# Layer 1 of a fused attention and feed-forward kernel: features and attention take one ring of four PSUM banks, and the second products come one chunk later

## The chip, the cores and the metric

The kernel runs on one core of one Trainium2 chip. The metric is the device time of one launch in microseconds (us); lower is better. TensorE is called PE here, its weight loads PEld, VectorE DVE, ScalarE ACT, GpSimd POOL, and SyncE, which issues the DMAs, SP.

## What is computed

Batch 4, 8 heads, 576 positions, head size 64, so 2304 tokens of width 512; both feed-forward layers are 512 to 2048 to 512.

```python
def attention(q, k, v):                 # per batch and head, m = 32 landmarks
    q_lm, k_lm = means of q, k over 18 neighbouring positions
    A  = softmax(q @ k_lm.T / 8)        # 576 x 32
    Bm = softmax(q_lm @ k_lm.T / 8)     # 32 x 32
    C  = softmax(q_lm @ k.T / 8)        # 32 x 576
    Z  = Bm.T / (norm1(Bm) * norminf(Bm) + 1e-6)
    for _ in range(6):
        Z = 2 * Z - Z @ Bm @ Z          # Newton steps towards the inverse
    return A @ Z @ C @ v

def layer1(x, w_in, w_out):             # x: heads side by side
    h = x @ w_in
    return (h * clip(h + 3, 0, 6) / 6) @ w_out

def layer2(x, w_in, w_out, a, b):
    h = x @ w_in
    P = a[0] + a[1]*h + a[2]*h**2 + a[3]*h**3
    Q = 1 + abs(b[0])*abs(h) + abs(b[1])*h**2
    return (P / (Q + 1e-6)) @ w_out

out = layer2(layer1(attention(q, k, v)))
```

## The kernel before, in words

**Weights.** They arrive as 64-bit floats. For each of 32 pieces ACT (L140) and DVE (L141 to L143) turn the bits into a 32-bit value, called `val`, and for 24 of the pieces ACT and POOL (`split`, L94 and L99) then divide it into a high and a low part. A product of two such split operands is three matmuls: high by high, high by low, low by high.

**Attention, batch by batch.** `scores_c` makes the scores of C and of Bm in four PSUM tiles (two tiles "end", two tiles "big"); DVE takes maxima (L295 to L299), makes the exponent's offset `nb` (L301), and ACT the exponentials (L307 for the big tiles). Then come transposes (`transpose_e`), the Newton steps (`first_e`, `first_v`, `newton`) and `tmat`, whose result is the small matrix `T`. `u_pair` multiplies `T` by the first layer's weights (L227) and keeps the split product `us` (L442, L443). `scores_a` and `soft_a1` to `soft_a3` make the softmax A, transposed and split, as the tile `AT`. Batch 0 goes through this ahead of layer 1; batches 1 to 3 go through it in the middle of layer 1 of the batch before.

**Layer 1.** The tokens are 8 blocks of 288; each block has 16 chunks of 128 features, 128 chunks in all. Three steps serve a chunk:

- `l1_in`: six matmuls of 288 columns (L467) into a PSUM tile `psh`; ACT makes relu(h + 3) (L470), DVE the product g (L472), which is the last reader of the PSUM tile.
- `l1_split`: ACT (L94) and POOL (L99) divide g into the tile `ghl`, 4 buffers.
- `l1_out`: twelve matmuls (L490) from `ghl` into the four accumulators `psy0` to `psy3` of the block, one bank each. When a block is done, ACT and DVE empty the four banks into `y` tiles (L514, L516, L518), of which there are 2 buffers, and DMAs store them.

**PSUM** has 8 banks here: four for `psy`, two that the attention takes in turn under the tag `psa`, and two that `l1_in` takes in turn under the tag `psh` (batch 0's attention uses both kinds). A tile waits until the last reader of the tile that had its bank before is done.

**Layer 2** works through 6 blocks of 384 tokens in an order written by hand.

**What sets the order.** Up to layer 2 every step is entered in a list with a place (`at(place, f)`); the list is sorted by place. Chunk n has `l1_in` at place n, `l1_split` at n + 1.1, `l1_out` at n + LEAD + 0.2. Buffers and banks of one tag are handed out in turn in this sorted order. A scheduler that works with its own model of the engines then decides in which order the instructions stand on each engine; each engine carries its own list out in that order, and an instruction that waits holds up those behind it.

```python
def at(place, f, *a):
    plan.append((place, len(plan), f, a))
...
for n in range(NCH):
    at(n, l1_in, n)
    at(n + 1.1, l1_split, n)
    at(n + LEAD + 0.2, l1_out, n)
```

Of the kernel before, what the change touches and what calls it, by code (L numbers as in the profile page):

```python
# [9 lines left out]
F32 = mybir.dt.float32  # L10
F32R = mybir.dt.float32r
# [14 lines left out]
P = 128  # L26
HB = S // 2
# [33 lines left out]
def fused(ctx: ExitStack, tc: tile.TileContext, qT, kT, v, w_in, w_out, w2_in, w2_out, ca, cb, out):  # L61
# [29 lines left out]
    def split(dst_hi, dst_lo, src, hi_eng, lo_eng):  # L91

        if hi_eng is A:
            A.activation(dst_hi, src, AF.Copy)  # L94
        elif hi_eng is G:
            G.tensor_scalar(dst_hi, src, 1.0, 0.0, op0=ALU.mult, op1=ALU.add)
        else:
            V.tensor_copy(dst_hi, src)
        lo_eng.tensor_tensor(dst_lo, src, dst_hi.bitcast(F32), op=ALU.subtract)  # L99
# [80 lines left out]
    w1p = pw1.__enter__()  # L180
# [3 lines left out]
    pp = ps_l1.__enter__()  # L184
# [6 lines left out]
    st = {}  # L191

    def psa(tag="psa"):
        return pp.tile([P, 512], F32, tag=tag, name=tag, bufs=2 if tag in ("psa", "psh") else 1)

    def load_kq(b, cut=1):
        kx[b] = att.tile([P, NPAIR, S + LM], F32, tag="kx", name="kx")
# [34 lines left out]
    def scores_a(b, h):  # L232
        sT = att.tile([P, 18, LM], F32, tag="sT", name="sT", bufs=1)
        pss = [psa("psh" if b == 0 else "psa") for _ in range(2)]
        by_head(
            pss, slice(0, HB),
            lambda r, a: kx[b][r:r + 64, a, S:S + LM],
            lambda r, a: qx[b][r:r + 64, a, h * HB:(h + 1) * HB],
        )
        for g in range(2):  # L240
            V.transpose(sT[:, 9 * g:9 * g + 9, :].rearrange("p a m -> p (a m)"), pss[g][:, :HB])
        st[b, h, "sT"] = sT
# [27 lines left out]
    def scores_c(b):  # L270

        qs = st.pop((b, "qs"))
        mx = att.tile([P, 2, 4], F32, tag="cmx", name="cmx", bufs=2)
        end = [psa() for _ in range(2)]
        by_head(
            end, slice(0, TN + LM),
            lambda r, a: qs[r:r + 64, a, :], lambda r, a: kx[b][r:r + 64, a, 512:S + LM],
        )
        if b == 0:
            far = end  # L280
            big = [psa("psh") for _ in range(2)]
        else:

            far = []
            for g in range(2):
                t = att.tile([P, TN + LM], F32, tag=f"ce{g}", name="ce", bufs=1)
                A.activation(t, end[g][:, 0:TN + LM], AF.Copy)
                far.append(t)
            big = [psa() for _ in range(2)]
# [158 lines left out]
    hps, ghl, yps = {}, {}, {}  # L448
# [8 lines left out]
    def l1_in(n):  # L457
        blk, c = turn[n]
        b, h = divmod(blk, 2)
        at = AT[b, h]  # L460
        f0 = (c % 4) * P
        ps = pp.tile([P, 512], F32, tag="psh", name="psh", bufs=2)
        k = 0
        for g in range(2):
            u = U[b, c // 4, g]
            for wp, xp in ((0, 0), (0, 1), (1, 0)):
                PE.matmul(ps[:, :HB], u[:, wp, f0:f0 + P], at[:, xp, g, :], start=(k == 0), stop=(k == 5))  # L467
                k += 1
        r = w1p.tile([P, HB], F32, tag="r", name="r")
        A.activation(r, ps[:, :HB], AF.Relu, bias=three)  # L470
        gg = w1p.tile([P, HB], F32, tag="g", name="g")
        V.scalar_tensor_tensor(gg, in0=r, scalar=6.0, in1=ps[:, :HB], op0=ALU.min, op1=ALU.mult)  # L472
        hps[n] = gg

    def l1_split(n):
        gg = hps.pop(n)
        t = w1p.tile([P, 2, HB], F32R, tag="ghl", name="ghl", bufs=4)
        split(t[:, 0, :], t[:, 1, :], gg, A, G)
        ghl[n] = t

    def l1_out(n):
        blk, c = turn[n]
        c0, c1 = (0, NFC - 1) if blk > 1 else (c - c % HC, c - c % HC + HC - 1)
        if c == c0:
            yps[blk] = [pp.tile([P, 512], F32, tag=f"psy{e}", name="psy") for e in range(NDC)]
        ps, t = yps[blk], ghl.pop(n)
        o = (c % 2) * DM
        for e in range(NDC):
            for i, (wp, xp) in enumerate(((0, 0), (0, 1), (1, 0))):
                PE.matmul(  # L490
                    ps[e][:, :HB], w1[c // 2][wp][:, o + e * P:o + (e + 1) * P], t[:, xp, :],
                    start=(c == c0 and i == 0), stop=(c == c1 and i == 2),
                )
        if c == c1 and c1 < NFC - 1:
            part[blk] = [slab.tile([P, GW], F32, tag="slab", name="ypart") for i in range(2)]
            for e in range(NDC):
                y = part[blk][e // 2][:, (e % 2) * HW:(e % 2) * HW + HB]
                if e % 2 == 0:
                    A.activation(y, ps[e][:, :HB], AF.Copy, scale=1.0 / 6.0)
                else:  # L500
                    V.tensor_scalar(y, ps[e][:, :HB], 1.0 / 6.0, None, op0=ALU.mult)
        elif c == c1:
            ps = yps.pop(blk)
            yd[blk] = dram.tile([P, NDC, HB], F32, name=f"yd{blk}")
            for e in range(NDC):
                if blk == 2 * B - 1 and e >= 2:
                    if e == 2:
                        y2 = w1p.tile([P, 2, HB], F32R, tag="ghl", name="y2", bufs=4)
                    y = y2[:, e - 2].bitcast(F32)
                else:  # L510
                    y = w1p.tile([P, HB], F32, tag="y", name="y")
                if blk in part:
                    y0 = part[blk][e // 2][:, (e % 2) * HW:(e % 2) * HW + HB]
                    V.scalar_tensor_tensor(y, in0=ps[e][:, :HB], scalar=1.0 / 6.0, in1=y0, op0=ALU.mult, op1=ALU.add)  # L514
                elif e % 2 == 0:
                    A.activation(y, ps[e][:, :HB], AF.Copy, scale=1.0 / 6.0)  # L516
                else:
                    V.tensor_scalar(y, ps[e][:, :HB], 1.0 / 6.0, None, op0=ALU.mult)  # L518
                SP.dma_start(yd[blk][:, e], y)
# [61 lines left out]
    def at(place, f, *a):  # L581
        plan.append((place, len(plan), f, a))
# [55 lines left out]
            at(n0 + 19.5 + 4 * u, u_pair, b, u)  # L638

    NCH = 2 * B * NFC  # L640
    LEAD = 3
    L2P = {}

    def open_l2():
# [11 lines left out]
# [4 lines that stand above are left out]
    at(NCH - 30, open_l2)  # L660
# [180 lines left out]
```

## Time and profile before

| | us |
|---|---|
| median of 3 runs (870.58, 873.90, 874.69) | 873.9 |
| the profiled execution's own time | 875.29 |
| its span, first to last instruction | 873.5 |
| PE busy within the span | 834.2 |
| DVE busy | 577.2 |
| POOL busy | 483.2 |
| ACT busy | 474.9 |

The sums of the prediction are made against the profiled execution, 875.29 us, which lies 1.4 us above the median of the runs. A busy PE is not yet a PE at its peak: matmuls overlap in a pipeline, so the time that one adds to a stream of its kind is read from how far apart their starts are. In a row of a timeline the bracket at the end is the idle time of the engine before it and what ended that idle time.

### The profile page before, as it was taken

The numbers are of one execution on the slowest core, as the hardware profiler recorded it, in microseconds if no ns is written. First come the engines' busy times: TensorE is split into PE (matmuls) and PEld (weight loads), VectorE is DVE, ScalarE is ACT, GpSimd is POOL, SyncE is SP. The second block draws the span as 40 slices with busy tenths as digits, with TensorE's granted clock in tenths as the row PEclk, the third lists the DMA queues.
The fourth block names the chain that finished last, engine by engine and source line by source line (L and its number), as shares of the span: only waits on it lengthen the run. The fifth ranks groups of instructions, "written<-read, shape, count | busy, mean of one in ns | idle before, by whom it ended". The sixth has DMA issues, their size and how long they took to land.

```text
span 873.5 us, 14948 instructions
## 1 busy us (share of the span) xinstructions
PE 834.2 (96%) x5766; PEld 748.6 (86%) x5766; DVE 577.2 (66%) x910; ACT 474.9 (54%) x876; POOL 483.2 (55%) x353
## 2 busy tenths in 40 slices
PE   9679989999999899998999999999999999999998
PEld 8558879788977789888999899898998998989986
DVE  6967895776576945766215876765766666666566
ACT  3434654465445634655434666565665655656564
POOL 1438364465345533577331886766676685675542
PEclk9768999999999999999999999999999999999999
DMA  9765464669148740595797010010010010000000
GB/s 354 275 226 168 147 229 167 225 201 334 38 158 287 253 163 28 189 327 197 262 324 254 1 37 8 30 37 1 37 37 1 37 36 1 37 1 1 37 1 36
DMA packets 46310, 113.16 MB, mean 130 GB/s; under 512 B 6176, under 2 KB 14368, under 8 KB 45856
## 3 DMA queue, kind: packets, MB, share of 16 engines
q1 hardware_dynamic: 46240, 112.22, 36.7%
q8 instruction: 45, 0.74, 0.3%
q14 instruction: 25, 0.20, 0.1%
HBM read 81.79 MB, written 30.41 MB: 128 GB/s over the span
## 4 chain that ended last, share of the span: by engine, by line
PE 66%; DVE 15%; DMA 6%; ACT 6%; issue 4%; POOL 2%; SPq 0%; DVEq 0%; ACTq 0%; POOLq 0%
PE po L740 20%; PE ph L687 20%; PE psy L490 14%; PE psh L467 7%; DMA raw<-in_moe_w_out 3%; DVE val L142 2%; DVE val L143 2%; PE psa L227 2%; DMA qx<-in_q 2%; DVE g L472 1%; ACT val L140 1%; PE psa L410 1%; DVE val L141 1%; DMA yr<-yd 1%; DMA yd<-y 1%
## 5 line engine op out<-in xcount | busy, mean ns | idle before, releaser
L490 PE MATMUL psy<-ghl,whi 128*128 128x288 f32 x1024 | 225.3, 304 | 6.7 <-POOL ghl L99 4.4
L99 POOL TENSOR_TENSOR ghl<-g,ghl 128x288 fp32r<-128x288 f32 x128 | 127.4, 999 | 151.8 <-ACT ghl L94 143.1
L740 PE MATMUL po<-w2s,g2hl 128*128 128x512 f32 x864 | 209.6, 396 | 1.5 <-POOL g2hl L99 1.5
L687 PE MATMUL ph<-yhl,w2s 128*128 128x384 f32 x1152 | 208.5, 336 | 0.6 <-DVE y L518 0.6
L687 PEld LDWEIGHTS ph<-yhl,w2s 128*128 128x128 f32 x1152 | 202.1, 188 | 4.5 <-DVE y L518 0.8
L740 PEld LDWEIGHTS po<-w2s,g2hl 128*128 128x128 f32 x864 | 161.3, 188 | 37.9 <-POOL g2hl L99 2.9
L490 PEld LDWEIGHTS psy<-ghl,whi 128*128 128x128 f32 x1024 | 169.7, 191 | 16.9 <-issue 7.3
L490 PE MATMUL psy<-ghl,wlo 128*128 128x288 f32 x512 | 150.4, 299 | 0.0
L467 PE MATMUL psh<-AT,us 128*128 128x288 f32 x768 | 134.7, 308 | 12.5 <-DVE g L472 11.4
L467 PEld LDWEIGHTS psh<-AT,us 128*128 128x128 f32 x768 | 112.9, 194 | 25.5 <-DVE g L472 16.3
L717 DVE SCALAR_TENSOR_TENSOR q<-q,r 128x768 f32<-128x768 f32 (+1 forms) x52 | 46.6, 896 | 114.2 <-ACT r L712 114.2
L699 POOL TENSOR_SCALAR q<-t,cb_s 128x768 f32<-128x768 f32 x44 | 56.5, 1283 | 100.9 <-ACT t L697 100.9
L99 POOL TENSOR_TENSOR g2hl<-g,g2hl 128x768 fp32r<-128x768 f32 (+1 forms) x52 | 89.7, 1726 | 32.4 <-ACT g2hl L94 32.4
L472 DVE SCALAR_TENSOR_TENSOR g<-r,psh 128x288 f32<-128x288 f32 x128 | 56.8, 448 | 73.4 <-ACT r L470 65.2
L94 ACT ACTIVATE ghl<-g 128x288 fp32r<-128x288 f32 x128 | 56.2, 442 | 83.1 <-DVE g L472 75.9
L490 PEld LDWEIGHTS psy<-ghl,wlo 128*128 128x128 f32 x512 | 97.8, 191 | 0.9 <-issue 0.9
L470 ACT ACTIVATE r<-psh,three 128x288 f32<-128x288 f32 x128 | 63.1, 498 | 56.8 <-PE psh L467 56.6
L711 ACT ACTIVATE r<-q,lnb 128x768 f32<-128x768 f32 (+1 forms) x52 | 46.2, 889 | 81.8 <-POOL q L700 76.3
L99 POOL TENSOR_TENSOR wlo<-val,whi 128x1024 fp32r<-128x1024 f32 x24 | 59.9, 2496 | 52.1 <-ACT whi L94 48.9
L700 POOL TENSOR_TENSOR q<-q,t 128x768 f32<-128x768 f32 x44 | 84.5, 1920 | 3.7
L697 ACT ACTIVATE t<-ph 128x384 f32<-128x384 f32 x96 | 46.9, 489 | 56.5 <-PE ph L687 55.9
L718 DVE SCALAR_TENSOR_TENSOR p<-p,ca_s,r 128x768 f32<-128x768 f32 (+1 forms) x52 | 64.6, 1243 | 0.0
(144 smaller groups left out, 1016.3 us busy)
## 6 DMA issues: line engine op xcount, KB each, us to landing
raw<-in_moe_w_in SPq DMA_DIRECT2D x32, 512.0 KB, 5.9
raw<-in_moe_w_out SPq DMA_DIRECT2D x32, 512.0 KB, 5.3
wis<-wid SPq DMA_DIRECT2D x24, 512.0 KB, 7.4
w2s<-w2di SPq DMA_DIRECT2D x16, 512.0 KB, 6.0
w2s<-w2do SPq DMA_DIRECT2D x16, 512.0 KB, 5.9
yd<-y SPq DMA_DIRECT2D x32, 144.0 KB, 2.9
out<-o SPq DMA_DIRECT2D x18, 256.0 KB, 2.0
vx<-in_v SPq DMA_DIRECT2D x4, 1024.0 KB, 8.5
```

What stands on the lines that cost most here:

```text
L94: A.activation(dst_hi, src, AF.Copy)
L99: lo_eng.tensor_tensor(dst_lo, src, dst_hi.bitcast(F32), op=ALU.subtract)
L467: PE.matmul(ps[:, :HB], u[:, wp, f0:f0 + P], at[:, xp, g, :], start=(k == 0), stop=(k == 5))
L470: A.activation(r, ps[:, :HB], AF.Relu, bias=three)
L472: V.scalar_tensor_tensor(gg, in0=r, scalar=6.0, in1=ps[:, :HB], op0=ALU.min, op1=ALU.mult)
L490: PE.matmul(ps[e][:, :HB], w1[c // 2][wp][:, o + e * P:o + (e + 1) * P], t[:, xp, :], start=(c == c0 and i == 0), stop=(c == c1 and i == 2),)
L687: PE.matmul(ps[i][:, :T2], w2i[u][wp][:, d * 256 + i * P:d * 256 + (i + 1) * P], yh[:, xp, d, :], start=(k == 0), stop=(k == 11),)
L697: A.activation(t[:, i], h, AF.Abs)
L699: eng.tensor_scalar(q[:, cs], t[:, cs], cb_s[:, 1:2], cb_s[:, 0:1], op0=ALU.mult, op1=ALU.add)
L700: eng.tensor_tensor(q[:, cs], q[:, cs], t[:, cs], op=ALU.mult)
L718: V.scalar_tensor_tensor(p, in0=p, scalar=ca_s[:, 0:1], in1=r, op0=ALU.add, op1=ALU.mult)
L740: PE.matmul(ops[j][m], t[:, xp, i, m * P:(m + 1) * P], w2o[u][wp][:, i * DM:(i + 1) * DM], start=(c == 0 and k == 0), stop=(c == NFC - 1 a ...
```

## The change

Three edits. The tiles that were tagged `psa` and `psh` now share one tag, `psx`, with 4 banks, taken in turn by all of them in the order of the sorted list. `LEAD` is 4 in place of 3, so that `l1_out` of a chunk stands one place later. The tag `ghl` has 5 buffers in place of 4.

```diff
     def psa(tag="psa"):
-        return pp.tile([P, 512], F32, tag=tag, name=tag, bufs=2 if tag in ("psa", "psh") else 1)
+        return pp.tile([P, 512], F32, tag="psx" if tag in ("psa", "psh") else tag, name=tag, bufs=4 if tag in ("psa", "psh") else 1)
...
-        ps = pp.tile([P, 512], F32, tag="psh", name="psh", bufs=2)
+        ps = psa("psh")
...
-        t = w1p.tile([P, 2, HB], F32R, tag="ghl", name="ghl", bufs=4)
+        t = w1p.tile([P, 2, HB], F32R, tag="ghl", name="ghl", bufs=5)
...
-                        y2 = w1p.tile([P, 2, HB], F32R, tag="ghl", name="y2", bufs=4)
+                        y2 = w1p.tile([P, 2, HB], F32R, tag="ghl", name="y2", bufs=5)
...
-    LEAD = 3
+    LEAD = 4
```

The number of instructions on each engine is the same; their order is not, since the scheduler sees other waits. Two places follow.

PE in the start of the program, from batch 0's second pair of transposes to the first Newton step (`warm` are matmuls without a use, L379 is `first_v`, L368 `first_e`, L398 and L401 `newton`, and L227 from qx and kx is `scores_a` of batch 0). Before:

```order
L357 MATMUL psy_315<-ident,e 128x128 x4
L379 MATMUL psh<-vx,eT 32x64 x16
L227 MATMUL psh<-qx,kx 32x288 x4
L379 MATMUL psh<-vx,eT 32x64 x4
L227 MATMUL psh<-qx,kx 32x288 x4
L592 MATMUL warm<-bm_281 128x128 x11
L368 MATMUL psa<-bm_281 128x128 x2
L379 MATMUL psh<-vx,eT 32x64 x20
L592 MATMUL warm<-bm_281 128x128 x4
L398 MATMUL psn<-ev 128x128
```

In the changed kernel:

```order
L357 MATMUL psy_315<-ident,e 128x128 x4
L592 MATMUL warm<-bm_281 128x128 x11
L368 MATMUL psa<-bm_281 128x128 x2
L379 MATMUL psh<-vx,eT 32x64 x20
L227 MATMUL psh<-qx,kx 32x288 x4
L592 MATMUL warm<-bm_281 128x128 x4
L227 MATMUL psh<-qx,kx 32x288 x4
L398 MATMUL psn<-ev 128x128
L379 MATMUL psh<-vx,eT 32x64 x20
```

Both halves of `scores_a` moved from ahead of `first_e` to behind it; the second half now takes the bank that the first `first_e` tile had.

ACT around the exponentials of batch 1 (L307), in layer 1 of batch 0 (L470 are the relus of single chunks, L94 with `ghl` the high parts, L499 empties an accumulator, L442 evicts `u_pair`). Before:

```order
L140 ACTIVATE val<-raw 128x1024
L307 ACTIVATE e,csm<-psa,cnb 128x512
L308 ACTIVATE e,csm<-ce,cnb 128x64
L307 ACTIVATE e,csm<-psa,cnb 128x512
L308 ACTIVATE e,csm<-ce,cnb 128x64
L470 ACTIVATE r<-psh,three 128x288 x2
L94 ACTIVATE ghl<-g 128x288 x2
L442 ACTIVATE us<-psa 128x512 x2
```

In the changed kernel:

```order
L470 ACTIVATE r<-psh,three 128x288 x2
L499 ACTIVATE ypart<-psy 128x288 x2
L94 ACTIVATE ghl<-g 128x288
L307 ACTIVATE e,csm<-psa,cnb 128x512
L308 ACTIVATE e,csm<-ce,cnb 128x64
L307 ACTIVATE e,csm<-psa,cnb 128x512
L308 ACTIVATE e,csm<-ce,cnb 128x64
L94 ACTIVATE ghl<-g 128x288
L442 ACTIVATE us<-psa 128x512 x2
```

The exponentials now stand behind two relus and the emptying of a finished accumulator, and PE's `u_pair` (evicted by L442), which takes over the two big score banks, stands behind 8 matmuls of one `l1_out`, 2 of the next, two `l1_in` and 10 more of `l1_out`.

## Rows read from the trace of the kernel before

**Rows 1.** Windows, three stages: stretch and length, busy us (instructions) of PE, PEld, DVE, ACT, POOL; granted clock, DMA share, GB/s.

```profile
0.00:72.00 72.00, 56.59 (x472) 46.80 (x473) 56.89 (x105) 29.23 (x58) 28.56 (x30) 0.79 0.77 282
72.00:465.00 393.00, 374.38 (x3281) 339.09 (x3279) 245.39 (x436) 202.56 (x438) 196.88 (x164) 0.99 0.60 207
465.00:873.50 408.50, 403.28 (x2016) 362.76 (x2016) 274.89 (x370) 243.14 (x380) 257.78 (x160) 1.00 0.08 28
```

**Rows 2.** Chain that ended last, in order of time: start, us, what.

```profile
413.13 1.59 PE psy L490 x12
415.52 1.59 PE psy L490 x12
...
504.77 4.19 PE po L740 x18
```

**Rows 3.** Waits of PE from 72 to 465: total us, times, longest.

```profile
PE psh L467 <- DVE g L472: 7.2, 9, 2.1
PE psy L490 <- POOL ghl L99: 4.4, 4, 2.1
```

**Rows 4.** Timeline of PE, the longest waits: start, us, what, idle before.

```profile
201.57 0.66 PE L467 MATMUL psh<-AT,us 128*128 128x288 f32 x3 [1.40 <-DVE g L472]
...
256.77 1.06 PE L467 MATMUL psh<-AT,us 128*128 128x288 f32 x6 [1.81 <-DVE g L472]
...
284.23 0.54 PE L490 MATMUL psy<-ghl,whi 128*128 128x288 f32 x2 [1.52 <-ACT y L516]
...
296.98 1.09 PE L467 MATMUL psh<-AT,us 128*128 128x288 f32 x3 [2.15 <-DVE g L472]
...
399.47 0.61 PE L490 MATMUL psy<-ghl,whi 128*128 128x288 f32 x1 [2.07 <-POOL ghl L99]
```

**Rows 5.** Windows of 20 us, columns as in rows 1.

```profile
280.00:300.00 20.00, 16.33 (x117) 14.71 (x117) 14.27 (x21) 11.52 (x29) 10.40 (x7) 0.92 0.67 242
...
400.00:420.00 20.00, 20.00 (x144) 20.00 (x143) 9.93 (x14) 10.09 (x19) 14.83 (x12) 0.93 0.66 233
```

**Rows 6.** Timeline of PE in the start of the program.

```profile
26.80 0.81 PE L227 MATMUL psh<-qx,kx 64*32 64x288 f32 x8 [1.78 <-DVE sT L241]
...
57.20 2.77 PE L467 MATMUL psh<-AT,us 128*128 128x288 f32 x10 [0.75 <-ACT us L442]
...
67.36 3.25 PE L467 MATMUL psh<-AT,us 128*128 128x288 f32 x12 [4.23 <-DVE g L472]
70.41 1.37 PE L490 MATMUL psy<-ghl,whi 128*128 128x288 f32 x5
```

**Rows 7.** Timeline of DVE in the start of the program.

```profile
32.82 1.45 DVE L141 TENSOR_SCALAR val<-val 128x1024 uint32<-128x1024 uint32 x1
...
36.53 0.74 DVE L254 TENSOR_REDUCE sm<-sT 128x18 f32<-128x576 f32 x1
37.20 1.75 DVE L347 TENSOR_SCALAR rc<-rc 128x2 f32<-128x2 f32 x1
...
40.38 0.60 DVE L370 SCALAR_TENSOR_TENSOR ev<-psa,rc,ident 128x128 f32<-128x128 f32 x2
```

**Rows 8.** Timeline of POOL in the start of the program.

```profile
31.66 2.07 POOL L248 TENSOR_TENSOR sT<-sT,mx 128x576 f32<-128x576 f32 x1 [3.08 <-DVE mx L247]
36.58 2.34 POOL L99 TENSOR_TENSOR wlo<-val,whi 128x1024 fp32r<-128x1024 f32 x1 [2.85 <-ACT whi L94]
...
43.55 1.41 POOL L99 TENSOR_TENSOR AT<-aT,AT 128x576 fp32r<-128x576 f32 x1 [1.87 <-ACT AT L94]
```

**Rows 9.** Timeline of PE, scores of batch 1 and the next `u_pair`.

```profile
88.28 1.09 PE L227 MATMUL psa<-kx,qs 64*32 64x512 f32 x16
...
97.61 1.11 PE L227 MATMUL psa<-val,T 64*32 64x256 f32 x32
```

**Rows 10.** Timeline of ACT, second large exponential of batch 1.

```profile
95.31 0.68 ACT L307 ACTIVATE e<-psa,cnb 128x512 f32<-128x512 f32 x1
```

**Rows 11.** Timeline of DVE at the end of the fourth block.

```profile
284.19 0.46 DVE L518 TENSOR_SCALAR y<-psy 128x288 f32<-128x288 f32 x1 [4.24 <-DMA yd<-y]
```

## The prediction

> **What bounds the kernel.** I read the windows by stage first. From 465 us on, in layer 2, PE is busy 403.3 of 408.5 us, and up to 72 us it has little to do [rows 1]. In layer 2 the chain of waits is PE after PE, 18 matmuls every 4.19 us [rows 2]; its order is written by hand, so those 408 us stay. What can move lies ahead of 465 us. From 72 to 465 us PE is busy 374.4 of 393 us, DVE 245, POOL 197, ACT 203 [rows 1]: PE sets the pace, at 0.133 us a matmul (12 take 1.59 us, and 2.39 us part two starts, so a chunk is 1.6 us of products and 0.8 us of features) [rows 2]. The reader is to see that at most the 18.6 idle us, and what the clock loses after them, are to be won there.
>
> Then the waits of PE in that stage: features wait 7.2 us, in nine places, until DVE's g gives a bank back, and products wait 4.4 us for POOL's low part [rows 3]. Four single waits carry most of that, and a fifth, 1.52 us, is for an accumulator to be emptied [rows 4]. Behind two of them the granted clock of a 20 us window falls to 0.92 and 0.93 [rows 5]: PE ran at 2.4 GHz, stood for 2.15 and 2.07 us [rows 4], and for a part of what followed had 1.2 GHz. At either level that is read as (1 - 0.92) x 20 = 1.6 us and 1.4 us lost.
>
> **The change, part by part.** No instruction is added or taken away, and no DMA. What changes is how long PE can go on when another engine is late. Before, between the end of a chunk's features and the next use of its bank lie two products and one chunk's features, 30 matmuls or 4.0 us; products follow three chunks behind. Now, where attention takes no tile, four products and three features lie between, 66 matmuls or 8.8 us, and products have one chunk, 2.4 us, more time. Where attention takes two tiles per chunk, as in the Newton steps, four banks reach only to the next chunk but one or less, about 2.4 us, less than before. So the two halves of the stage go different ways.
>
> *A, the start.* Half of batch 0's A scores, done at about 27.6 us before [rows 6], now need a bank that `first_e` holds until DVE evicts it, at about 41 us [rows 7]. So the softmax work on DVE and POOL moves from before the Newton steps into them. One reduction of 0.74 us leaves DVE's path to `first_e`, and POOL's 2.07 us subtraction, beside which a 1024-wide operation took 1.45 us [rows 7, 8], goes too. I take 2 us off the start of the Newton steps, give 0.5 us back within them, and get -1.5 us at the first products (70.41 us) [rows 6]. In POOL's list batch 1's three additions (L218) now all stand ahead of the first low part; I cost that at nothing, because the first g comes late anyway, and at about 2 us, by the like-sized subtraction [rows 8], if it comes early. The gain's end is the whole 4.23 us wait [rows 6]. The other end: from 27.6 us to the end of POOL's split at 44.96 us the chain took 17.4 us [rows 8]; started at 41 us it would end at 58.4 us, 1.2 us after the first features (57.20) [rows 6], and with DVE shared by the Newton steps up to +3 us.
>
> A rule speaks against this term. An update of rc, 128x2 numbers, took 1.75 us beside POOL's 2.34 us split [rows 7, 8]. The Trainium skill (SBUF — State Buffer, Terms, shared port pair) has VectorE and GpSimd locking one pair of ports for a whole instruction; now that split falls on the last step before `first_e`, and by the rule the term would be about 0 in place of -1.5 us.
>
> *B, batch 1's exponentials.* PE's `u_pair` takes the banks of the big scores, and its cover is 32 matmuls, 4.3 us. The big scores ended at 89.37 us [rows 9], the second large exponential at 96.0 us [rows 10], 6.6 us later; before, 8.2 us passed until `u_pair` [rows 9], so nothing waited. Now PE waits 6.6 - 4.3 = 2.3 us, and the next products stand behind that wait; as after 2.15 us at 296.98, the clock may fall, 1.6 us [rows 4, 5]. Sum +3.0 us, with a little under half of that for a fall that isn't certain. Ends: 0 (ACT comes earlier) and 6.6 + 1.6 = +8.2 us (the exponentials, now behind the emptying of an accumulator that ends with those 32 matmuls, leave no cover).
>
> *C, features of blocks 3 and 4.* The waits at 201.57 (1.40 us) and 256.77 (1.81 us) [rows 4]: the first goes, since the conversions are spread over more chunks there, and half the second, -2.3 us. Ends -3.2 and 0.
>
> *D, end of block 4.* DVE stood 4.24 us for the store of `y` [rows 11] and everything behind it came late: 1.52 us for the accumulator, then 2.15 us for g [rows 4]. Now more work lies between the accumulator's last and next use (0.8 us by the order), and both features that follow are ahead; the second wait and its clock loss go. -0.8 - 2.15 - 1.6 = -4.5 us. Ends -5.3 (all of the three) and 0.
>
> *E, end of block 6.* POOL is late by a burst of layer 2 splits. With 2.4 us more in hand the 2.07 us wait and about 1 us of smaller ones go (4.4 in all in the stage) [rows 3, 4], and the clock's 1.4 us [rows 5]: -4.4 us. Ends -4.5 and 0, if the burst only grows.
>
> *F, new waits.* In the Newton steps of batches 1 to 3, and at three block ends where the order leaves 0.6 to 1.0 us less before the emptied accumulator is used: nothing in the trace shows them; bounds 0 and three times 2.3 us as in B, +6.9. I take +2 us, nearer to the small end, because the features' g mostly comes within the cover left.
>
> The fifth buffer of `ghl` adds no instruction; it holds the chunk that the later products leave open, and without it POOL's low part would wait one chunk, 2.4 us, sooner. Sum: -1.5 + 3.0 - 2.3 - 4.5 - 4.4 + 2.0 = -7.7 us from 875.29 us, which is 867.6 us: **868 us**, 0.7% under the median of 873.9 us.
>
> **The rivals.**
>
> *Nothing is won.* DVE and POOL carry bursts of conversions that take as long as before; a deeper ring only lets PE run ahead and stand later, and in the busy stretches it isn't deeper at all, so the change doesn't do what it says. For it: 7.2 us of waits come only with late g, and a bank isn't their first cause [rows 3]. Against: between the bursts DVE has room, 245 of 393 us [rows 1]. Then A is 0, C -1, D and E -2 each, B and F +5: 875.3 us, by the median 874 us. The Trainium skill (TensorE: Matmul & The Clock Gate, HAM oscillation) tells of a kernel in which PSUM double-buffering on top of a steadily fed PE gave no further gain; by that rule the time stays.
>
> *Attention holds the features' banks.* In-order PE stands at each batch's exponentials until ACT and DVE have done the softmax. Place: `u_pair` behind the big scores of batch 1, and the features behind the transposes of batches 2 and 3. Price: 8.2 us once (B's end) and twice 4.2 us (the 6.6 us less a chunk's 2.4 us), 16.6 us. Against it stand C, D and E, -11.2 us, with A at 0: +5.4 us, 880 us. It decides the sign from 11.2 us of such waits on, and is over the bound below from about 14 us. For it: the long DVE list between two g in batch 1; against it: in batches 2 and 3 the order puts 4 us of products and more ahead of the transposes.
>
> *All waits go.* g's 7.2 and POOL's 4.4 us [rows 3], the clock's 3.0 us [rows 5], and no new ones: 14.6 us, 861 us.
>
> **How the numbers follow.** A measurement of this kernel can tell about 0.5% from no change, that is 869.5 to 878.3 us. Forecast (864 to 872 us) 0.42, nothing won (870 to 878 us) 0.27, attention holds the banks (876 to 886 us) 0.19, all waits go (856 to 864 us) 0.12. Four fifths of the forecast's chance and all of the last lie below 869.5 us: faster 0.46; same 0.33; slower 0.21, of which 0.16 is the second rival and 0.05 the first's upper edge with A at +3. The range, 859 to 880 us, leaves out the lowest part of the last case (0.04) and the upper half of the second rival (0.11); the forecast's own is 864 to 872 us.
>
> **What would show it.** Features' waits for g above 1 us at places like 201.57 and 296.98 us gone; the low part's wait near 399 us gone; no window after 280 us under 0.95 of the clock; the first products at 69 us; a new wait of 2 to 4 us of `u_pair` for ACT's exponential, near 95 us. Layer 2 must take 408 us as before. The forecast is wrong if the waits for g sum to 7 us again, if waits of PE for ACT's L307 or for DVE in the attention pass 10 us, or if the first products start after 72 us.

## The result, and the profile after

The changed kernel takes **861.32 us** (median of 4 runs, 858.74 to 862.70), the kernel before 874.30 us (4 runs, 870.58 to 874.74). The ratio of the runs is 0.9857 (95% interval 0.9822 to 0.9893): 1.4% faster. The profiled execution took 861.21 us, with a span of 859.4 us.

The windows by stage, with the end of layer 1 now at 450.9 us in place of 465 [rows 1]:

```profile
0.00:72.00 72.00, 56.37 (x481) 45.36 (x482) 58.88 (x110) 30.55 (x61) 30.58 (x31) 0.79 0.78 282
72.00:450.90 378.90, 368.79 (x3272) 337.38 (x3270) 235.47 (x431) 200.99 (x436) 195.81 (x162) 0.99 0.62 216
450.90:859.40 408.50, 403.27 (x2016) 362.54 (x2016) 274.87 (x370) 243.17 (x380) 258.01 (x160) 1.00 0.08 27
```

Layer 2 takes 408.5 us as before. Layer 1's stage is 14.1 us shorter; PE's idle time in it fell from 18.6 to 10.1 us, and its busy time by 5.6 us. Nine matmuls more lie ahead of 72 us, about 1.2 us at 0.133 us each; for the other 4 us of busy time there is no single row.

The waits of PE from 72 us to the end of layer 1, answering to [rows 3] (waited for: us in total, times, longest):

```profile
PE psa L227 <- DVE g L472: 5.3, 3, 2.0
PE psy L490 <- POOL ghl L99: 1.7, 3, 1.2
...
```

The wait of features for g, 7.2 us before, is not in the list any more. In its place `u_pair` (L227) waits for g: 5.3 us in three places. They stand in the timeline of PE, with the start of the program ahead of them and the longest wait for the low part behind, to be read beside [rows 6] and [rows 4]:

```profile
54.69 2.91 PE L467 MATMUL psh<-AT,us 128*128 128x288 f32 x10 [2.08 <-ACT us L442]
...
65.38 4.45 PE L467 MATMUL psh<-AT,us 128*128 128x288 f32 x17 [3.28 <-DVE us L443]
69.62 1.16 PE L490 MATMUL psy<-ghl,whi 128*128 128x288 f32 x4
...
93.61 1.07 PE L227 MATMUL psa<-val,T 64*32 64x256 f32 x16 [2.02 <-DVE g L472]
...
150.91 1.07 PE L227 MATMUL psa<-wis,T 64*32 64x256 f32 x16 [1.34 <-DVE g L472]
...
241.66 2.30 PE L227 MATMUL psa<-wis,T 64*32 64x256 f32 x32 [1.96 <-DVE g L472]
...
379.49 0.40 PE L490 MATMUL psy<-ghl,whi 128*128 128x288 f32 x1 [1.25 <-POOL ghl L99]
```

The new waits stand where one ring makes them possible: `u_pair` now takes the banks that features had, and waits until their g is done. What holds the g up is read from DVE's own list ahead of 241.66 us:

```profile
236.87 1.35 DVE L221 TENSOR_REDUCE qs<-qx 128x64 f32<-128x1152 f32 x1 [0.47 <-DMA qx<-in_q]
238.14 0.74 DVE L219 TENSOR_REDUCE kx<-half 128x64 f32<-128x576 f32 x1
238.80 0.68 DVE L141 TENSOR_SCALAR val<-val 128x1024 uint32<-128x1024 uint32 x1
239.40 1.84 DVE L99 TENSOR_TENSOR AT<-aT,AT 128x576 fp32r<-128x576 f32 x1
241.16 0.81 DVE L472 SCALAR_TENSOR_TENSOR g<-r,psh 128x288 f32<-128x288 f32 x2
```

ACT's two relus were done by 237.8 us; DVE then does the next batch's landmark sums, a conversion and the low part of an AT, with no time between them, before it comes to g at 241.16 us. The kernel before has the same list at this place, ahead of the features that waited 1.81 us at 256.77 us [rows 4]:

```profile
254.50 1.85 DVE L99 TENSOR_TENSOR AT<-aT,AT 128x576 fp32r<-128x576 f32 x1
256.28 0.80 DVE L472 SCALAR_TENSOR_TENSOR g<-r,psh 128x288 f32<-128x288 f32 x2
```

So this wait did not go with the change; it passed from the features to `u_pair`.

The list shows one thing more. The low part of AT took 1.84 and 1.85 us here, and 0.75 us where POOL stood idle when it began (e7, below). In the changed kernel POOL was adding at the same time:

```profile
238.96 1.66 POOL L218 TENSOR_TENSOR half<-kx 128x576 f32<-128x576 f32 x1 [2.48 <-DVE kx L219]
```

This is no single case. From 72 to 465 us of the kernel before, 34 operations of DVE took over 0.4 us longer than the shortest of the same line and shape, 30.3 us in sum, and each of the 34 ran beside an operation of POOL; of the other 401 half did. In the changed kernel's stage they are 27, with 23.8 us. One stands ahead of each of the three waits for g in [rows 4] (L338, 2.62 us at 197.60 us; AT's low part; L299, 2.34 us at 293.56 us), and neither the prediction nor an experiment went after them.

At the end of the fourth block, where DVE had stood 4.24 us for the store of `y` [rows 11], the same list now reads (the brackets give DVE's idle time):

```profile
276.41 0.46 DVE L518 TENSOR_SCALAR y<-psy 128x288 f32<-128x288 f32 x1 [2.07 <-PE psy L490]
276.78 1.10 DVE L141 TENSOR_SCALAR val<-val 128x1024 uint32<-128x1024 uint32 x1
277.80 0.44 DVE L472 SCALAR_TENSOR_TENSOR g<-r,psh 128x288 f32<-128x288 f32 x1
...
282.10 0.46 DVE L518 TENSOR_SCALAR y<-psy 128x288 f32<-128x288 f32 x1
```

The second `y` stands 5.7 us behind the first, with conversions and features' g between them, and DVE waits for no store; ACT still stands 1.18 us for one, at 281.65 us. PE shows no idle time at all from 270 to 300 us.

The clock moved too. Windows of 20 us (columns as in [rows 1]), of the three new places and of the two in [rows 5]:

```profile
80.00:100.00 20.00, 17.98 (x154) 14.00 (x153) 14.53 (x33) 9.56 (x29) 6.38 (x6) 0.91 0.66 211
140.00:160.00 20.00, 18.66 (x166) 16.40 (x167) 16.12 (x31) 10.02 (x21) 10.18 (x11) 0.91 0.70 254
240.00:260.00 20.00, 18.34 (x162) 15.63 (x163) 13.02 (x20) 10.95 (x22) 11.62 (x12) 0.91 0.46 159
280.00:300.00 20.00, 20.00 (x157) 17.66 (x156) 16.15 (x32) 11.87 (x29) 10.29 (x8) 1.00 0.94 335
...
400.00:420.00 20.00, 20.00 (x153) 20.00 (x152) 4.91 (x11) 8.67 (x21) 10.27 (x11) 1.00 0.88 304
```

The two falls of before are gone, and there is one behind each wait of `u_pair`. How far such falls are chance is the matter of the last section.

To place the gain, the matmuls of L467 and L490 were counted in both traces, and the times compared at which as many were done. Where a batch's attention is also done in both, at chunks 37, 64 and 96, the difference is the time won so far. The last four columns are the steps between.

| profiled execution | first features | to chunk 37 | 37 to 64 | 64 to 96 | 96 to the end | sum |
|---|---|---|---|---|---|---|
| the changed kernel | -2.5 | +1.2 | -0.6 | -8.4 | -3.8 | -14.1 |
| ring alone (e1) | -3.2 | +4.6 | -0.7 | -7.5 | -2.5 | -9.3 |
| later products alone (e2) | +0.6 | -1.4 | +1.1 | -6.5 | -1.2 | -7.4 |
| before, four `y` (e4) | -2.1 | +1.7 | -3.0 | -5.8 | -1.0 | -10.2 |
| changed, batches 2, 3 one later (e7) | -0.9 | -1.2 | -4.8 | -8.8 | -4.2 | -19.9 |
| before, batches 2, 3 one later (e9) | +0.4 | +2.3 | -1.4 | -1.0 | -1.1 | -0.8 |

Each row is one execution: the first column differs by up to 2.7 us even between kernels whose start is not changed (e2, e4 and e9, from -2.1 to +0.6), so a step of that size in it shows nothing. Counted a few matmuls earlier or later at chunk 37, up to 1.3 us passes between the two columns beside it. Chunk 37 is reached at 187.7 us in the changed kernel, 64 at 273.8 us and 96 at 369.8 us.

### The profile page after: what moved, and what is told of

It is laid out like the page before. It is cut to its first block, busy times and chain, and to the rows that moved or that the text cites. A ratio compares the mean times of both kernels' runs of the same rounds, so it can differ in the third digit from the quotient of the medians.

```text
span 859.4 us, 14955 instructions
## 1 busy us (share of the span) xinstructions
PE 828.4 (96%) x5766; PEld 745.3 (87%) x5766; DVE 569.2 (66%) x910; ACT 474.7 (55%) x876; POOL 484.4 (56%) x353
## 4 chain that ended last, share of the span: by engine, by line
PE 71%; DVE 11%; DMA 6%; issue 3%; POOL 3%; ACT 3%; SPq 1%; DVEq 0%; ACTq 0%; POOLq 0%
PE po L740 20%; PE ph L687 20%; PE psy L490 17%; PE psh L467 8%; PE psa L227 3%; DMA qx<-in_q 2%; DMA raw<-in_moe_w_out 2%; DVE val L142 2%; PE psa L410 1%; DVE val L143 1%; DMA yd<-y 1%; POOL ghl L99 1%; POOL q L700 1%; DMA w2do<-wlo 1%; DMA raw<-in_moe_w_in 1%
## 5 line engine op out<-in xcount | busy, mean ns | idle before, releaser
L490 PE MATMUL psy<-ghl,whi 128*128 128x288 f32 x1024 | 222.2, 304 | 2.5 <-POOL ghl L99 1.7
L490 PEld LDWEIGHTS psy<-ghl,whi 128*128 128x128 f32 x1024 | 168.7, 192 | 16.4 <-issue 4.8
L490 PE MATMUL psy<-ghl,wlo 128*128 128x288 f32 x512 | 150.6, 299 | 0.0
L467 PE MATMUL psh<-AT,us 128*128 128x288 f32 x768 | 128.7, 307 | 6.0 <-DVE us L443 3.3
L467 PEld LDWEIGHTS psh<-AT,us 128*128 128x128 f32 x768 | 112.4, 195 | 13.1 <-DVE us L443 4.2
L490 PEld LDWEIGHTS psy<-ghl,wlo 128*128 128x128 f32 x512 | 97.6, 191 | 0.0
L94 ACT ACTIVATE ghl<-g 128x288 fp32r<-128x288 f32 x128 | 56.1, 441 | 69.4 <-DVE g L472 67.5
L99 POOL TENSOR_TENSOR wlo<-val,whi 128x1024 fp32r<-128x1024 f32 x24 | 61.7, 2572 | 50.5 <-ACT whi L94 48.7
L470 ACT ACTIVATE r<-psh,three 128x288 f32<-128x288 f32 x128 | 62.6, 496 | 38.2 <-PE psh L467 37.7
```

Source lines behind the costliest of these rows:

```text
L490: PE.matmul(ps[e][:, :HB], w1[c // 2][wp][:, o + e * P:o + (e + 1) * P], t[:, xp, :], start=(c == c0 and i == 0), stop=(c == c1 and i == 2),)
```

## The experiments

The theory: the ring and the later products each let PE go on past a late DVE or POOL, and the gain is the old waits, less those of `u_pair`. The rivals: one of the two does it all, or only both together. Two cautions hold for all that follows. Each ratio is taken to runs of the kernel before that were made along with the experiment (medians 874.37, 874.33 and 875.61 us), so that versions are compared by their ratios. And every edit also gives the engines another order of instructions, so that a run shows what an edit and its order do together.

**The parts alone: e1 and e2.**

```diff
# e1: the changed kernel, with
-    LEAD = 4
+    LEAD = 3
-        t = w1p.tile([P, 2, HB], F32R, tag="ghl", name="ghl", bufs=5)
+        t = w1p.tile([P, 2, HB], F32R, tag="ghl", name="ghl", bufs=4)
# e2: the kernel before, with
-    LEAD = 3
+    LEAD = 4
-        t = w1p.tile([P, 2, HB], F32R, tag="ghl", name="ghl", bufs=4)
+        t = w1p.tile([P, 2, HB], F32R, tag="ghl", name="ghl", bufs=5)
```

> The ring of four banks alone; products three chunks behind and four ghl buffers as before. Theory 1 (ring and place of the products cover different late arrivals, so their gains add): the start's -2.5 us, and the waits of features for g near 201 and 297 us gone with one clock fall, but the wait for POOL's low part near 399 us (2.07 us and its clock fall) stays: 865 to 868 us. Theory 2 (only both together win, because PE has to run ahead in the features before the products can be late): 871 to 875 us. Theory 3 (the ring does it all): 861 to 863 us.

> Products four chunks behind with five ghl buffers; two and two banks as before. Theory 1: the low part's wait near 399 us and its clock fall gone, features' waits for g about 5 to 7 us as before, start as before: 868 to 871 us. Theory 2: 871 to 875 us. Rival (the later products do it all, because every wait for g is then hidden behind products): 861 to 864 us, features' waits for g under 3 us.

e1 took 867.13 us, ratio 0.9929 (0.9910 to 0.9949); e2 867.17 us, ratio 0.9916 (0.9903 to 0.9929). So each part alone wins, 0.7% and 0.8%, and the two together 1.4%: in the sum they add, as far as the intervals tell. Both rivals fall. The waits of PE from 72 to 451 us, of e1:

```profile
PE psy L490 <- POOL ghl L99: 3.7, 4, 1.5
PE psy L490 <- ACT ghl L94: 2.3, 2, 1.7
...
PE psa L227 <- DVE g L472: 1.4, 1, 1.4
```

and of e2:

```profile
PE psh L467 <- DVE g L472: 6.9, 7, 2.5
...
PE psy L490 <- POOL ghl L99: 1.0, 3, 0.5
```

Each part takes away its own wait: under the ring features no longer wait for g, and products wait 6.0 us for splits, POOL's and ACT's (4.4 us for POOL's before); with the later products the splits come in time, and features wait 6.9 us for g (7.2 before). e1 lies in the theory's range, e2 0.8 us below it. By stages, though, the parts don't simply add (the table): from chunk 64 to 96 either one wins 6.5 to 7.5 us and both 8.4. At the end of layer 1 they do, 2.5 and 1.2 us to 3.8; in e2 a feature there still waits 2.52 us for g (379.82 us), because its relu stands on ACT behind an operation that waited 4.18 us for layer 2's input. In the first 37 chunks the ring alone loses 4.6 us, of which a fall of the clock makes 3.4 (granted clock 0.83 from 100 to 120 us); that the later products would make this good is not shown.

**The fifth buffer: e3.**

```diff
# the changed kernel, with (also for y2)
-        t = w1p.tile([P, 2, HB], F32R, tag="ghl", name="ghl", bufs=5)
+        t = w1p.tile([P, 2, HB], F32R, tag="ghl", name="ghl", bufs=4)
```

> The changed kernel with four ghl buffers in place of five. The prediction's working says that the fifth buffer holds the chunk that the later products leave open: then the low part waits for the products of the chunk before it and PE waits for it often, 0.5 us or more in half of the 128 chunks, and the time is above 880 us. Rival: the scheduler's order already has the split of a chunk behind the products that free the buffer, with about 1.2 us of matmuls as cover: waits of PE for the low part 5 to 10 us in all, 864 to 870 us.

862.80 us, ratio 0.9871 (0.9856 to 0.9886); the changed kernel's is 0.9857 (0.9822 to 0.9893). The time lies below both expected ranges. PE's waits for the low part rose from 1.7 to 5.2 us, as the rival said, but no difference in time can be told: by the two ratios the fifth buffer is worth 1.2 us, and their intervals leave room from nothing to almost 5 us.

**The store of y: e4 and e5.**

```diff
# e4: the kernel before; e5: as e3; both with
-                    y = w1p.tile([P, HB], F32, tag="y", name="y")
+                    y = w1p.tile([P, HB], F32, tag="y", name="y", bufs=4)
```

> The kernel before with four y buffers in place of two, nothing else. The prediction's term D says that DVE's 4.24 us stand for the store of y at 284 us is the first cause of the 1.52 us and 2.15 us waits of PE behind it and of a clock fall of 1.6 us. If so, all of it goes: 4 to 5 us less, 869 to 870 us, DVE's wait for the store gone and no window under 0.95 of the clock from 280 to 300 us. Rival: DVE's list is full there, and without the store the same g comes late behind conversions: 873 to 875 us, the wait at 297 us still over 1 us.

> The changed kernel with four ghl buffers (which the third run showed to be worth 0 to 2 us) and four y buffers. Theory (the ring and the later products cover the very lateness that the y store makes, so that the two gains do not add): 858 to 862 us, DVE's wait for the store of y, 4.0 us in the changed kernel, gone without PE starting layer 2 earlier by more than 2 us. Rival (they add, 7 us of the run with four y buffers on top of 12 us): 853 to 856 us.

e4 took 867.26 us, ratio 0.9930 (0.9915 to 0.9945), 7 us less than before by the medians and 6 by the ratio, where term D had 4 to 5: the four buffers win at least what D gave to the store. But the path is not the one that D told, and the rival's mark came true too. In e4 PE has one wait over 0.5 us between 270 and 370 us, and the window around it keeps its clock:

```profile
293.46 1.06 PE L467 MATMUL psh<-AT,us 128*128 128x288 f32 x6 [2.04 <-DVE g L472]
```

```profile
280.00:300.00 20.00, 17.96 (x137) 17.68 (x136) 18.83 (x35) 13.86 (x33) 11.92 (x8) 1.00 0.81 259
```

So a wait for g like the 2.15 us at 296.98 [rows 4] stands there without the store too: DVE is busy 18.83 of 20 us in e4, and g comes late with or without it. Both times a small operation of DVE stands ahead of the g and runs beside POOL's split of a weight until that ends. Before:

```profile
293.56 2.34 DVE L299 TENSOR_TENSOR cmx<-cmx 128x2 f32<-128x2 f32 x1
293.49 2.38 POOL L99 TENSOR_TENSOR wlo<-val,whi 128x1024 fp32r<-128x1024 f32 x1 [0.50 <-ACT whi L94]
```

and in e4:

```profile
288.32 2.54 DVE L338 TENSOR_TENSOR bm<-bm,m 128x256 f32<-128x256 f32 x1
288.18 2.40 POOL L99 TENSOR_TENSOR wlo<-val,whi 128x1024 fp32r<-128x1024 f32 x1 [0.63 <-ACT whi L94]
```

The first of the two takes 0.15 us at 289.49 us in the changed kernel, the second 0.40 us at 304.30 us before. What went in e4 is the 1.52 us for the accumulator, a fall of the clock, and two waits in batch 3's attention, 0.54 us at 304.43 and 1.19 us at 311.55 in the trace of before. That the store makes more of these than the 1.52 us is not shown: the clock does not fall behind every such wait (last section), and ahead of the two waits another small operation of DVE took 2.32 us beside POOL (L325, 128x64, at 300.70 us).

e5 took 860.89 us, ratio 0.9845 (0.9820 to 0.9869), no faster than the changed kernel that can be told, nor than e3, from which it differs by the four `y` buffers alone. DVE's stand for the store, 3.67 us at 420.86 us in the changed kernel, went, and layer 1 ended 0.6 us earlier. So the two gains do not add: the change covers the lateness that four `y` buffers take away.

**Why u_pair waits: e6 and e7.**

```diff
# e6: the changed kernel, with
-        split(t[:, 0].rearrange(f), t[:, 1].rearrange(f), aT, A, G if b == 0 else V)
+        split(t[:, 0].rearrange(f), t[:, 1].rearrange(f), aT, A, G)
# e7: the changed kernel, with
-    d2=0,
+    d2=1,
```

> The changed kernel, with the low part of AT of batches 1 to 3 subtracted on POOL in place of DVE. In the changed kernel it stands 0.78 and 1.84 us in DVE's list right ahead of the g for which u_pair waits at 150.9 us (1.34 us) and 241.7 us (1.96 us), and the granted clock falls behind both. Theory (u_pair waits for a feature's bank because DVE's burst of attention work is ahead of g): both waits under 0.7 us, the clock's falls behind them mostly gone, 856 to 859 us. Rival (POOL is as full there, and features' low parts come later by the 1.4 us that such a subtraction takes): 861 to 865 us with more than 3 us of waits for POOL's low part.

> The changed kernel with the whole attention of batches 2 and 3 entered one chunk later. If u_pair's waits for g come from the attention's burst falling together with the emptying of a block's accumulators, they move away or shrink: 857 to 860 us. If the burst is the attention's own (landmark sums, low parts of AT and of us in a row on DVE), the waits move by about 2.4 us and stay: 860 to 863 us.

e6 took 861.63 us, ratio 0.9858 (0.9832 to 0.9884), no change, in the rival's range. The wait at 241.7 us is gone, and a larger one stands 3.7 us behind it:

```profile
245.37 0.40 PE L490 MATMUL psy<-ghl,whi 128*128 128x288 f32 x1 [2.62 <-POOL ghl L99]
```

POOL's list ahead of it:

```profile
237.77 1.44 POOL L99 TENSOR_TENSOR AT<-aT,AT 128x576 fp32r<-128x576 f32 x1 [0.58 <-ACT AT L94]
239.66 1.67 POOL L218 TENSOR_TENSOR half<-kx 128x576 f32<-128x576 f32 x1 [0.45 <-DVE kx L219]
241.29 2.29 POOL L218 TENSOR_TENSOR half<-qx 128x576 f32<-128x576 f32 x1
243.54 2.55 POOL L99 TENSOR_TENSOR ghl<-g,ghl 128x288 fp32r<-128x288 f32 x2
```

The theory is right about DVE's list (the g came in time at 241 us), and the rival is right about the price: POOL's additions for the landmarks are pushed back, and two low parts come behind them. At 150 us the wait stayed (1.42 us), against the theory.

e7 took **855.44 us**, ratio 0.9793 (0.9766 to 0.9820), the fastest version of all and below the theory's range; 0.65% under the changed kernel by the two ratios, whose intervals only just lie apart. There `u_pair` waits as follows at this place (PE), with DVE's list ahead of it:

```profile
239.56 1.07 PE L227 MATMUL psa<-wis,T 64*32 64x256 f32 x16 [0.55 <-DVE g L472]
```

```profile
239.06 0.44 DVE L472 SCALAR_TENSOR_TENSOR g<-r,psh 128x288 f32<-128x288 f32 x1
239.42 0.75 DVE L99 TENSOR_TENSOR AT<-aT,AT 128x576 fp32r<-128x576 f32 x1
```

The g now stands ahead of AT's low part, and the wait is 0.55 us in place of 1.96. Two smaller waits of the changed kernel from chunk 37 to 64 are also gone, 0.59 us at 195.48 and 0.33 us at 200.84 us. With the fall of the clock behind 241.66 us (0.91 of 20 us, 1.8 us), which e7 has not, they make 4.1 of the 4.2 us more in that step. The fall is the part that may be chance: e3 has a wait of 2.04 us at 241.51 us and no fall behind it, and e7 has no window under 0.97 from 80 to 460 us, though its waits at 94.78 and 151.59 us are as long as the changed kernel's. AT's low part is also shorter, 0.75 us, with POOL idle when it began. Whether the emptying of the accumulators is what the place avoids is not shown: what is seen is the order of DVE's list.

**Is the place good by itself? e9, e10, e11.**

```diff
# e9: the kernel before; e10: the changed kernel, also d1=5.17 for d1=4.17; both with
-    d2=0,
+    d2=1,
# e11: the changed kernel, with
-    d2=0,
+    d2=2,
```

> The kernel before (two and two banks, products three chunks behind) with the attention of batches 2 and 3 entered one chunk later, as in the seventh run. Theory (the place is good only for the ring, where u_pair and features wait for each other's banks): 872 to 877 us. Rival (one chunk later moves the attention's burst on DVE away from the emptying of accumulators, whatever the banks): 866 to 870 us, as much as the 6 us that the seventh run won on the changed kernel.

> The changed kernel with the attention of all of batches 1 to 3 entered one chunk later. The wait of 2.02 us at 94 us is that of a u_pair of batch 0 for a feature's g, which on DVE stands behind conversions and batch 1's maxima. If batch 1's scores make it, by taking four banks at that place, it goes or moves, and the gain of 5.3 us that the first 11 chunks lose there comes back in part: 851 to 855 us. Rival (batch 1's burst only moves with its wait, and the stage ends with batch 3): 855 to 858 us.

> The changed kernel with the attention of batches 2 and 3 entered two chunks later in place of one. If the seventh run's gain comes from leaving the block's end, a second chunk keeps it: 853 to 857 us, with u_pair's wait near 240 us under 1 us. Rival (u_pair of the next batch then comes too close to the features that need it, and PE waits for us): 857 to 865 us with waits of features for us (L443) at the block starts near 175 and 270 us.

e9 took 874.69 us, ratio 0.9989 (0.9975 to 1.0003): on the kernel before the place is worth nothing that can be told, as the theory said. Its gain in e7 needs the change; whether the ring or the later products, no run tells.

e10 took 861.89 us, ratio 0.9845 (0.9829 to 0.9860). The 2.02 us wait at 94 us went, and batch 1 has another in its Newton steps, for the result of `first_v`, which ACT evicts (L385):

```profile
126.36 0.59 PE L410 MATMUL psa<-ev 128*128 128x192 f32 x2 [2.33 <-ACT ev L385]
```

The rival (the burst moves with its wait) describes it, at a price above its range, and so above the theory's too.

e11 took 866.25 us, ratio 0.9891 (0.9869 to 0.9914): the second chunk gives back at least what the first one won. Neither the theory nor the rival fits, in time or mechanism; no wait of features for `us` appears at the block starts. In its place a tile of batch 2 waits for a feature's g, and later the low part is late:

```profile
201.15 0.49 PE L368 MATMUL psa<-bm 128*128 128x128 f32 x2 [1.76 <-DVE g L472]
...
392.52 0.40 PE L490 MATMUL psy<-ghl,whi 128*128 128x288 f32 x1 [1.74 <-POOL ghl L99]
```

**More of the same: e8.**

```diff
# the changed kernel, with
-    LEAD = 4
+    LEAD = 5
```

> The changed kernel with products five chunks behind in place of four, five ghl buffers as they are. Theory 1 (ring and place of the products cover different late arrivals): only waits for the low part can go, of which 1.7 us are left, so 859 to 862 us, with u_pair's waits for g (5.3 us) as they are. Rival (each further chunk of lead is worth the 7 us of the second run): 853 to 856 us.

862.45 us, ratio 0.9868 (0.9843 to 0.9893), no different from the changed kernel and just above the theory's range. A fourth chunk of lead found late low parts to cover; a fifth, with the five `ghl` buffers as they are, wins nothing. In its trace `u_pair`'s waits for g are not the 5.3 us that the theory left in place but one of 2.5 us, and new ones stand in batch 1's attention. Whether a sixth buffer would help was not tried.

## Why the prediction was right, and where it was not

The forecast was 868 us; measured were 861.3 us, inside the range and 0.8% under the forecast, but outside the forecast's own 864 to 872 us. The direction was right; the gain, 14.1 us between the two profiled executions, is nearly twice the 7.7 us of the sum, and a range of 21 us helped to hold it. The time is that of the rival "all waits go", but not by its mechanism: 10.1 us of waits remain, 5.3 of them new. By terms, with the table:

- **A, the start**, -1.5 us: at the term's own mark, the first products, -0.8 us (69.62 us, where 70.41 stood and 69 was said), with five more of the features' matmuls ahead of them, about 0.7 us; at the first features -2.5 us. DVE's reduction and POOL's subtraction left the path as told. The scatter between executions is as large as these numbers, so the size is not shown. The update of rc, 128x2 numbers, took 2.30 us beside POOL's split of 2.97 us and ended with it (37.66 and 37.64 us), where the two updates of the same size just before it took 0.15 and 0.16 us. The Trainium skill (SBUF — State Buffer, Terms, shared port pair) has the two engines lock each other out, and the trace agrees. Whether the term is then about 0, as the prediction drew from the rule, or -1.5 us, the scatter does not let one tell.
- **B, batch 1's exponentials**, +3.0 us: +1.2 measured to chunk 37, and **the step that says what PE waits for is wrong**. "PE waits 6.6 - 4.3 = 2.3 us" for ACT's exponential: PE did stand 2.02 us at 93.61 us with a fall of the clock behind it, but for a feature's g, which DVE ended at 93.56 us. The big scores can't be the tiles it took over, as the section on the change has it: ACT's exponentials still read their banks at 94.20 and 95.20 us. So the banks are not handed out strictly in turn at that place. I had followed which attention tile takes over which attention tile's bank, and not that the ring hands `u_pair` a feature's bank first. Batch 1's softmax is behind this wait all the same, one step further back. ACT stood 3.39 us for batch 1's offsets, with the relus that g needs behind them:

```profile
91.89 0.32 ACT L312 ACTIVATE eb<-ce,cnb 128x32 f32<-128x32 f32 x1 [3.39 <-DVE cnb L302]
...
92.52 0.87 ACT L470 ACTIVATE r<-psh,three 128x288 f32<-128x288 f32 x2
...
94.20 0.70 ACT L307 ACTIVATE e<-psa,cnb 128x512 f32<-128x512 f32 x1
```

The wait of 1.34 us at 150.91 us and a second fall of the clock belong to the step to chunk 37 as well. The other terms:

- **C, features of blocks 3 and 4**, -2.3 us: -0.6 measured. The features' two waits went, as said. What the term left out is the same thing: `u_pair` waits 1.96 us at 241.66 us, for the g at the place of DVE's list where features had waited, with a fall of the clock behind it. My second rival had attention hold the features' banks; the features held attention's, three times: 5.3 us of waits and three falls of the clock of about 1.5 us (priced below), 9.8 us where the rival had 16.6.
- **D, end of block 4**, -4.5 us: -8.4 from chunk 64 to 96, outside the term's ends. **This is the term that was mis-sized.** The 1.52 us wait, of which I let 0.8 go, went whole, as did the 2.15 us and the clock's 1.6: 5.3 us, the far end. Behind them the waits in batch 3's attention went as well, 0.54 and 1.19 us, which I had put under F as places for losses only; the last 1.4 us of the 8.4 have no single row. With four `y` buffers on the kernel before (e4) this step is 5.8 us shorter, but it keeps a wait of 2.04 us for g where D let the 2.15 us go with the store; in both traces the row ahead of that g is a small operation of DVE beside POOL's split.
- **E, end of block 6**, -4.4 us: -3.8. One wait of 1.25 us stays at 379.49 us, and the window from 400 us has its clock back. By its waits this is the later products' work, as the term has it: the low part's are 1.0 us with them alone, and 3.7 us with the ring alone. By time it is not so plain: this step is -1.2 us in e2, with the feature's wait of 2.52 us and a fall of the clock in it (0.92 from 380 to 400 us), and -2.5 us in e1.
- **F, new waits**, +2.0 us: from chunk 64 to 96 the trace has no wait of PE over 0.5 us. At the block ends one of 0.53 us stands at 420.94 us. The new waits are those of `u_pair`, which belong to B and C.

The fifth buffer of `ghl`, said to keep POOL from waiting a chunk sooner, is worth nothing that can be measured (e3). The Trainium skill (TensorE: Matmul & The Clock Gate, HAM oscillation) tells of one kernel in which PE kept its higher clock and PSUM double-buffering gave no further gain; the first rival made that its rule. It did not carry over: this PE stood 18.6 us in the stage, with two banks of each kind, and four shared ones alone gave 0.7%.

## What to carry to other kernels

When two users of banks or buffers are put into one ring, write out for each tile whose bank it takes over, and ask how late that one's last reader is: the new wait stands at the user that now follows the late one, and the places of the work have to be set again for the ring (e7 wins 0.65% more by one number, which on the kernel before is worth nothing that can be told). Different covers of the same lateness don't add: four `y` buffers gave 6 to 7 us on the kernel before and nothing that can be measured on the changed one, so look for the first cause before adding gains up. Where the tile's last reader is DVE, look too at what POOL does beside it: here an operation that POOL's held up stood ahead of each of the three longest waits for g in the kernel before. What it would be worth to place POOL's work elsewhere is not shown.

## What was not expected of the hardware

**The clock does not fall behind every such wait.** The wait of `u_pair` at 94 us is the same in the changed kernel and in e6, 2.02 and 2.00 us, with the same matmuls behind it. Windows of the changed kernel, columns as in [rows 1]:

```profile
94.00:96.00 2.00, 2.00 (x24) 1.52 (x13) 0.72 (x2) 2.00 (x8) 0.80 (x1) 0.82 0.91 222
96.00:98.00 2.00, 2.00 (x12) 1.65 (x15) 1.55 (x5) 1.13 (x4) 0.80 (x1) 0.50 0.93 250
```

and of e6:

```profile
94.00:96.00 2.00, 2.00 (x21) 1.73 (x14) 0.39 (x2) 2.00 (x9) 0.81 (x1) 1.00 0.83 213
96.00:98.00 2.00, 2.00 (x25) 1.25 (x25) 1.89 (x7) 1.33 (x4) 0.81 (x1) 1.00 1.03 339
```

In the first the clock is at 0.50 (1.2 of 2.4 GHz), and the matmuls from the wait to the next transpose (L357) take from 93.61 to 99.18 us, 5.57 us; in the second from 93.28 to 97.33 us, 4.05 us. The fall costs 1.5 us, near the 1.6 us that the prediction read from a window. Of four executions with this wait (the changed kernel, e6, e7, e11) one shows the fall. The prediction counted a whole fall in D and in E, and not quite half a fall in B; by these four traces it is a chance with each wait, and probably a part of the scatter between runs (the changed kernel's fastest, 858.74 us, has a mean granted clock of 0.986, the other three, 861.21 to 862.70 us, 0.976 to 0.978).
